# A Strassen-Winograd feed-forward layer on one core: three of the seven first-layer products of the last two groups as two-level units

## The chip, the core and the metric

The kernel runs on one core of a Trainium2 chip. The metric is device time in microseconds (us), from the first to the last instruction of one execution, as the median of several runs. The engines are named as the profile names them: PE (TensorE, with PEld for its weight loads), DVE (VectorE), ACT (ScalarE), POOL (GpSimd) and SP (the queue that issues most DMAs).

## What is computed

Eight images of 576 tokens go through an efficient attention (softmax of q over its features, of k over the tokens), then a Fourier mix, a layer norm and a feed-forward block:

```python
q_s = softmax(q, axis=-1); k_s = softmax(k, axis=2)
x = q_s @ (k_s^T v)                           # heads joined: (8, 576, 512)
u = x + real(fft(fft(x, axis=1), axis=2))
un = (u - mean) / sqrt(var + 1e-06)
out = u + relu(un @ w_ch1) @ w_ch2            # 512 -> 2048 -> 512
```

All arithmetic on the chip is in float32. The change touches only `relu(un @ w_ch1)`, the first layer, and what stands around it.

## The kernel before

**Groups and orders.** The 4608 tokens are cut into nine groups of 512: groups 0 to 7 are 512 tokens of one image each, group 8 has the left-over tokens of all images. They go through the feed-forward block one after the other, in the order 0 to 6, then 8, then 7. The place in that order is called the order: order 0 is computed plainly, orders 1 to 8 by a Strassen-Winograd scheme of seven products instead of eight. The attention and the Fourier mix of the next image run beside the feed-forward block of the present one, so during orders 1 to 6 PE, DVE, ACT and POOL have work of both. During order 7 only the layer norm of the last group is left, and during order 8 nothing.

**First layer (`up`, L1527 on).** The transposed normalized tokens `unT` (512 features by 512 tokens) and the weights are cut into 2 x 2 blocks. `unT` has seven slots: four raw blocks and three sums, made by DVE and POOL (L1396, L1400, L1405). The weights have seven slots per 128 rows, combined once at the start, kept in DRAM as eight tensors `w1s0` to `w1s7`, and loaded anew for each order, 896 KB at a time, into a ring of four places in `big` (`load`, L476). The loop over `j` takes four quarters of the 2048 columns; for each quarter come seven products in the order 1, 6, 5, 7, 2, 4, 3 (`ORDER`), each of four matmuls of 128 x 128 weights and 256 columns (L1544; the trace has two records for each float32 matmul, so a product shows as x8). Products add up in three PSUM banks `ba`, `bb`, `bc`. `strassen` (L1492) takes them out: ACT copies the first (L1515), DVE makes the sums `u2`, `u3` (L1514) and the four results (L1555), ACT applies the ReLU (L1551, L1556). At the end of a quarter `a_side` (L405 to L408) makes the four sums that the second layer needs: on POOL for orders 1 to 6, on DVE for orders 7 and 8. The results stand in `big`, in seven slots per row block; `hpairs` and `hblock` address them.

**Second layer (`deep_down`, L1641 to L1695, for orders 2 to 8).** Its products are two-level: product 1 and, in order 8, products 2 and 4 are single ones of 256 columns (L1641), the others are units of seven products of 128 columns (L1671), with operands made by `a_step` (L1617), sums taken out at L1678, L1685 and L1692, and results added to the output rows by `into` (L1621) and `sums` (L1624). `into` and `sums` run on POOL for orders 2 to 6, on DVE for 7 and 8 (`E`). The five `into` that follow the last unit, (5, 3), reach into the next order's first layer. The weights of the units, `w2d`, come in loads of 1024 KB.

**What sets the order of work.** Each step is a function with a planned time; all are sorted by it, and each engine issues its own instructions in that order. An engine that waits holds up all that stands behind it on that engine. The planned times are no clock: an instruction whose inputs are there starts at once. One planned unit is 0.87 us.

Of the kernel before, what the change touches and what calls it, by code (L numbers as in the profile page):

```python
# [40 lines left out]
F32 = mybir.dt.float32  # L41
# [78 lines left out]
def at(t, script):  # L120
    return [(t + dt, step) for dt, step in script]
# [17 lines left out]
class _Block:  # L139
    def __init__(self, ctx, tc, q, kT, v, w1, w2, ft, cd, out):  # L140
# [43 lines left out]
        d = self.dram  # L184
        self.w1s = [d.tile([P, 7, HD], F32, tag=f"w1s{p}", name=f"w1s{p}", bufs=1) for p in range(NP)]
        self.w2s = d.tile([7, P, NP, HD], F32, tag="w2s", name="w2s", bufs=1)
# [3 lines left out]
        for at in range(1, B + 1):  # L190
            self.base[at] = len(self.plan)
            self.plan += [self.w1s[p][:].rearrange("p a n -> p (a n)") for pair in PAIRS for p in pair]
# [59 lines left out]
    def flat(self):  # L252
        return self.turned().rearrange("p r n -> p (r n)")
# [163 lines left out]
    def combine(self, layer, p):  # L417
# [19 lines left out]
        if layer == 0:  # L437
            ops = ((4, ALU.add, 2, 3), (2, ALU.subtract, 0, 2), (5, ALU.subtract, 4, 0), (6, ALU.subtract, 1, 5))
            engines, times = (nc.vector,) * 4, (0, 0.4, 0.8, 1.2)
            to, first, second = self.w1s[p][:], slice(0, 2), slice(2, 3)  # L440
            one, two = halves(w[:, p, :]), quarter(3).unsqueeze(1)
# [1090 lines left out]
    def up(self, order, g):  # L1532

        nc, V = self.nc, self.nc.vector
        steps = []
        base, e = self.base[order], V if order >= B - 1 else nc.gpsimd
        for j in range(NP // 2):
# [25 lines left out]
            t = 2 * len(ORDER) * j  # L1563
            steps += at(t, job) + [(t + 2 * len(ORDER) - 0.5 + 5 * i * (j < NP // 2 - 1), lambda n=base + 2 * j + i: self.used(n)) for i in range(2)]
        return steps

# [24 lines left out]
    def deep_down(self, g, order):  # L1591
# [26 lines left out]

        def into(u, d, m):
            x = self.xs[g, u][:, :, d * HD:(d + 1) * HD].rearrange("p c (e n) -> p c e n", n=P)  # L1620
            E.tensor_tensor(out=x, in0=x, in1=tile(m), op=ALU.add)  # L1621
# [58 lines left out]
        def ends(unit, n):  # L1680
# [14 lines left out]
            if n == 3:  # L1695
# [3 lines left out]
                 (7, 6): [(1, sums, 6, 1), (3, into, 0, 1, 6), (5, sums, 7, 6), *(((7, into, 1, 0, 7), (9, into, 1, 1, 7)) if last else ())],  # L1699
                 (5, 3): [(0.6, into, 1, 1, 5), (1.2, into, 0, 1, 5), (1.8, into, 0, 1, 3)] if last else  # L1700
                         [(4, into, 1, 0, 7), (5.5, into, 1, 1, 7), (7, into, 1, 1, 5), (8.5, into, 0, 1, 5), (10, into, 0, 1, 3)]}
# [132 lines left out]
def kernel(ctx: ExitStack, tc: tile.TileContext, q, kT, v, w1, w2, ft,  # L1834
                                                           cd, out):
    blk = _Block(ctx, tc, q, kT, v, w1, w2, ft, cd, out)

    def timed(t, order, g):
        b = order + 1
# [92 lines left out]
    for order, g in enumerate(groups[1:], 1):  # L1932
        later += timed(t, order, g)
        t += UP + (TWICE if order > 1 else UP)
    steps += [(before + scale * t, step) for t, step in later]
# [58 lines left out]
```

## Time and profile before

| what | us |
|---|---|
| median of 3 runs (lowest, highest) | 1006.81 (1006.33, 1007.28) |
| the profiled execution, first to last instruction | 1006.6 |
| PE busy in it | 995.6 |
| DVE / ACT / POOL busy in it | 718.6 / 493.2 / 442.9 |
| first layer of order 7, start to start of its second layer | 815.03 to 863.51 |
| first layer of order 8, start to start of its second layer | 908.37 to 956.72 |

The page of the profile shows no other time of the profiled execution than its span. A row of the timeline gives the start, the duration, the engine, the line, the operation with output and input, its shape and count, and, in brackets, how long the engine had been idle and what ended that. Matmuls overlap in their pipeline, so the time that a product costs is read from the distance of two starts, not from its duration.

### The profile page before, as it was taken

Reading aid. Unit: us, or ns where it says so; the run is one execution under the profiler, and the core shown is the slowest. Engines: PE = TensorE matmul, PEld = TensorE weight load, DVE = VectorE, ACT = ScalarE, POOL = GpSimd, SP = SyncE. Lnnn points to the kernel's source line nnn. Section 1 sums busy time; section 2 is a strip of 40 time slices with the busy share of each in tenths; the row PEclk is TensorE's granted clock in tenths of the full one; section 3 lists DMA queues with packets and bytes.
Section 4 is the critical chain, followed back from the end, with each engine's and each line's share of the span. In section 5 each row is a group of like instructions: output and inputs, shape, how many; then the busy total and the mean of one; then the engine's idle time right before and its main releaser. Section 6 shows DMA issues by size and latency. Waiting matters only on the chain.

```text
span 1006.6 us, 19808 instructions
## 1 busy us (share of the span) xinstructions
PE 995.6 (99%) x7562; PEld 855.7 (85%) x7562; DVE 718.6 (71%) x1356; ACT 493.2 (49%) x1277; POOL 442.9 (44%) x445
## 2 busy tenths in 40 slices
PE   8999999999999999999999999999999999999998
PEld 6844464888888899889988998899889998998897
DVE  6898898666765887588756877688667945685563
ACT  4585642872468228832775177625772342151200
POOL 4263420357535637664655465655646450040000
PEclk9999999999999999999999999999999999999999
DMA  9987499687989666975677577847753765674573
GB/s 300 258 281 245 158 240 346 205 243 226 342 283 272 230 230 219 266 237 210 251 220 242 206 269 237 253 174 270 231 204 135 267 213 200 224 265 172 183 256 132
DMA packets 123559, 236.37 MB, mean 235 GB/s; under 512 B 24184, under 2 KB 88440, under 8 KB 112840
## 3 DMA queue, kind: packets, MB, share of 16 engines
q1 hardware_dynamic: 123096, 234.58, 71.0%
q8 instruction: 60, 0.98, 0.4%
q14 instruction: 35, 0.29, 0.1%
q10 hardware_dynamic: 288, 0.26, 0.1%
q0 software_dynamic: 80, 0.26, 0.1%
HBM read 199.94 MB, written 39.06 MB: 237 GB/s over the span
## 4 chain that ended last, share of the span: by engine, by line
PE 87%; DVE 7%; ACT 3%; DMA 1%; issue 1%; SPq 0%; POOL 0%; DVEq 0%; POOLq 0%
PE bb L1544 16%; PE ba L1544 11%; PE bc L1544 11%; PE bb L1671 10%; PE ba L1671 7%; PE bc L1671 7%; PE bb L1641 5%; PE bc L1479 2%; PE bb L1760 2%; PE two L840 2%; PE one L755 2%; PE two L1207 1%; PE two L1264 1%; PE ba L1479 1%; PE bc L1760 1%; PE ba L1760 1%
## 5 line engine op out<-in xcount | busy, mean ns | idle before, releaser
L1544 PE MATMUL bb<-unT,big 128*128 128x256 f32 x768 | 183.3, 380 | 0.0
L1544 PEld LDWEIGHTS bb<-unT,big 128*128 128x128 f32 x768 | 144.8, 190 | 20.7 <-DVE u L1514 0.7
L1556 ACT ACTIVATE big<-big 128x512 f32<-128x512 f32 x96 | 59.8, 629 | 147.6 <-DVE big L1555 141.0
L1544 PE MATMUL ba<-unT,big 128*128 128x256 f32 x512 | 123.9, 382 | 0.0
L1544 PE MATMUL bc<-unT,big 128*128 128x256 f32 x512 | 121.5, 380 | 0.1
L817 ACT ACTIVATE qT<-q 32x128 f32<-32x128 f32 x384 | 117.9, 307 | 5.9 <-DVE q L807 0.8
L1544 PEld LDWEIGHTS bc<-unT,big 128*128 128x128 f32 x512 | 96.9, 190 | 13.7 <-DVE big L1555 0.5
L1544 PEld LDWEIGHTS ba<-unT,big 128*128 128x128 f32 x512 | 95.5, 190 | 13.9 <-issue 0.5
L1514 DVE TENSOR_TENSOR u<-bb,s 128x512 f32<-128x512 f32 x66 | 45.2, 685 | 85.0 <-PE bb L1544 66.5
L1671 PE MATMUL bb<-big 128*128 128x128 f32 x848 | 103.8, 276 | 0.2 <-DVE u L1678 0.2
L1671 PEld LDWEIGHTS bb<-big 128*128 128x128 f32 x848 | 98.9, 192 | 1.0 <-DVE u L1678 1.0
L1390 POOL COPY unT<-unT 32x256 f32<-32x256 f32 x98 | 42.0, 428 | 90.2 <-DVE unT L1382 85.9
L1621 POOL TENSOR_TENSOR x<-x,big 128x512 f32<-128x512 f32 x45 | 60.9, 1368 | 46.0 <-DVE big L1678 19.7
L1617 DVE TENSOR_TENSOR big<-big 128x512 f32<-128x512 f32 x98 | 79.9, 842 | 0.0
L1671 PE MATMUL ba<-big 128*128 128x128 f32 x640 | 79.0, 276 | 0.0
L1671 PEld LDWEIGHTS ba<-big 128*128 128x128 f32 x640 | 75.0, 192 | 0.8
L1390 ACT COPY unT<-unT 32x256 f32<-32x256 f32 x126 | 50.7, 402 | 31.3 <-DVE unT L1382 29.5
L804 POOL TENSOR_TENSOR q<-q,qm 128x512 f32<-128x512 f32 x24 | 25.8, 1073 | 88.2 <-DVE qm L799 53.1
L405 POOL TENSOR_TENSOR big<-big 128x512 f32<-128x512 f32 x24 | 30.4, 1268 | 68.4 <-ACT big L1556 68.4
L1641 PE MATMUL bb<-big 128*128 128x256 f32 x256 | 58.3, 379 | 0.0
L1555 DVE TENSOR_TENSOR big<-bc,u 128x512 f32<-128x512 f32 x64 | 44.0, 688 | 17.3 <-PE bc L1544 16.4
L1641 PEld LDWEIGHTS bb<-big 128*128 128x128 f32 x256 | 48.0, 190 | 6.1
(336 smaller groups left out, 1917.9 us busy)
## 6 DMA issues: line engine op xcount, KB each, us to landing
big<-w2d SPq DMA_DIRECT2D x67, 1024.0 KB, 4.6
big<-w1s SPq DMA_DIRECT2D x64, 896.0 KB, 4.7
big<-w2s SPq DMA_DIRECT2D x16, 1024.0 KB, 4.8
big<-in_w_dram SPq DMA_DIRECT2D x21, 512.0 KB, 6.0
w2d<-big SPq DMA_DIRECT2D x42, 256.0 KB, 6.5
kb<-in_kT_dram SPq DMA_DIRECT2D x28, 320.0 KB, 7.8
q<-in_q_dram SPq DMA_DIRECT2D x28, 256.0 KB, 6.0
vt<-in_v_dram SPq DMA_DIRECT2D x84, 80.0 KB, 2.7
```

Source lines behind the costliest of these rows:

```text
L405: e1.tensor_tensor(out=to(4), in0=at(2), in1=at(3), op=ALU.add)
L817: nc.scalar.activation(to[t, i * Q:i * Q + Q], one, ACT.Exp)
L1390: copy(to, of)
L1514: plus = lambda t: V.tensor_tensor(out=temp(t), in0=box["bb"][:], in1=box["s1"][:], op=ALU.add)
L1544: nc.tensor.matmul(bank()[:, i, :], lhsT=w[:, WA_AT[m], k * P:(k + 1) * P], rhs=self.unT[g][:, B_AT[m], k, :], start=first and i == 0 and ...
L1555: steps = [(0, lambda: V.tensor_tensor(out=hp(i), in0=bank()[:], in1=u()[:], op=ALU.add)), (0.8, lambda: nc.scalar.activation(hp(i), hp(i) ...
L1556: (0.8, lambda: nc.scalar.activation(hp(i), hp(i), ACT.Relu))]
L1617: e.tensor_tensor(out=to(o), in0=to(x), in1=to(y), op=op)
L1621: E.tensor_tensor(out=x, in0=x, in1=tile(m), op=ALU.add)
L1641: nc.tensor.matmul(box[name][:, i, :], lhsT=h[p][:, A_AT[m], i * P:(i + 1) * P], rhs=self.stream[n][:, p, :], start=p == 0 and (m != 1 or ...
L1671: nc.tensor.matmul(box[place[n]][:, i, :], lhsT=own(m)(A_AT[n])[:, f, :], rhs=w[:, r // 2, r % 2 * P:r % 2 * P + P], start=first and f == ...
L1760: nc.tensor.matmul(bank()[:, i, :], lhsT=h[p][:, A_AT[m], i * P:(i + 1) * P], rhs=w[:, p, :], start=first and i == 0 and p == 0, stop=p == ...
```

## The change

In orders 7 and 8 the first layer is written out anew (`wide_up`).

- Products 1, 6, 7, 5 stay as they were, quarter by quarter, in this order and each in a PSUM bank of its own (`ba`, `bb`, `one`, `bc`).
- Products 2, 3 and 4 are computed for all four quarters at once, each as a unit of a second Strassen-Winograd level (`wide_unit`): seven products of four matmuls with 128 columns. The three units stand behind the four products of the first quarter, and the other three quarters follow them.
- The right sides of a unit, blocks of 128 x 128, need four small subtractions on DVE (`minus`), which read and write SBUF alone. Each unit has five additions from PSUM on DVE (`plus`) and two copies on ACT. Its four results go into slots 5, 6 and 4 of the hidden layer and are added later, by POOL (`more`) or DVE.
- The left sides of the units are loaded once, in the second layer of order 6, from DRAM into tiles that the attention no longer needs (`kb`, `q`, `F`, `ft`, `cd`, `ZT`, `vt`, `qT`, `T`): seven DMAs on SP, 3 MB in all. Their four sums for each unit are made once (`wide_sums`): unit 2's on DVE at the end of order 6, those of units 3 and 4 on POOL in the first layer of order 7, eight additions of 128 x 512.
- The side sums for the second layer run half on DVE, half on POOL (the last quarter's on DVE).
- The five `into` behind order 7's last unit go from DVE to POOL.
- The eight tensors `w1s0` to `w1s7` become one DRAM tensor, in which the part of one `p` has a longer stride between partitions.

The core of the diff:

```diff
+SHORT = (1, 6, 7, 5)
+UNIT, WIDE_AT = 7.2, {2: 5, 3: 6, 4: 4}
+WIDE = 3 * UNIT + 2 * len(SHORT) * (NP // 2)
...
+        self.w1c = d.tile([P, NP, 7, HD], F32, tag="w1s", name="w1s", bufs=1)
+        self.w1s = [self.w1c[:, p] for p in range(NP)]
...
-        base, e = self.base[order], V if order >= B - 1 else nc.gpsimd
+        base, e = self.base[order], nc.gpsimd
+        if order >= B - 1:
+            return self.wide_up(order, g)
...
+    def wide_sums(self, m, e, *times):
+        def make(o, x, y, op):
+            w = self.wide[m]
+            e.tensor_tensor(out=w[o], in0=w[x], in1=w[y], op=op)
+        some = (4, 2, 3, ALU.add), (5, 4, 0, ALU.subtract), (2, 0, 2, ALU.subtract), (6, 1, 5, ALU.subtract)
+        return [(t, lambda a=a: make(*a)) for t, a in zip(times, some)]
...
+    def wide_unit(self, g, m, *at_sums):
+        raw = lambda i: self.unT[g][:, B_AT[m], i // 2, i % 2 * P:i % 2 * P + P]
+        b_at = lambda i: raw(i) if i in (0, 2, 3) else some[:, (4, 1, 5, 6).index(i), :]
+        to = lambda i: self.hblock(WIDE_AT[m], i % 2, 1 - i // 2)
+        place = {1: "ba", 2: "ba", 6: "bb", 4: "bb", 5: "bc", 3: "bc", 7: "one"}
+        def minus(o, x, y):
+            V.tensor_tensor(out=b_at(o), in0=raw(x), in1=raw(y) if y < 4 else b_at(y), op=ALU.subtract)
+        def product(n):
+            for j in range(4):
+                nc.tensor.matmul(box[name][:, j, :], lhsT=self.wide[m][A_AT[n]][:, j, :], rhs=b_at(B_AT[n]),
+                                 start=first and j == 0, stop=True, skip_group_check=True)
+        def ends(n):
+            if n == 1:
+                nc.scalar.copy(temp("s1"), box["ba"])
+            if n == 6:
+                plus(temp("u2"), "bb", "s1")
+            if n == 7:
+                plus(temp("u3"), "one", "u2")
+                plus(to(3), "bc", "u3")
+            if n == 2:
+                nc.scalar.copy(to(0), box["ba"])
+            if n == 4:
+                plus(to(2), "bb", "u3")
+            if n == 3:
+                plus(to(1), "bc", "u2")
+        steps = [(t, lambda o=o, x=x, y=y: minus(o, x, y))
+                 for t, (o, x, y) in zip(at_sums, ((4, 1, 0), (5, 3, 4), (1, 3, 1), (6, 2, 5)))]
...
+            if j == 0:
+                put(1.9, lambda: nc.scalar.copy(hp(0), box["ba"]))
+                put(3.9, lambda: plus(temp("u2"), "bb", own(0)))
+                put(5.9, lambda: plus(hp(1), "one", got("u2")))
+                put(7.9, lambda: plus(hp(3), "bc", own(1)))
+                put(8.7, lambda: plus(hp(2), "bc", got("u2")))
...
+                put(12.7, more, G, 0, own(0), 2)
+                put(15.5, more, G, 2, own(2), 3)
+                put(22.6, more, G, 1, own(1), 4)
+                put(25.2, side, V, 4, 2, 3, ALU.add)
+                put(25.3, side, V, 2, 0, 2)
+                put(26, side, G, 5, 4, 0)
+                put(26.1, side, G, 6, 1, 5)
...
+        t = 2 * len(SHORT)
+        steps = part(0, 0) + at(t, self.wide_unit(g, 2, -3.05, -3, -1.3, -1.2))
+        for m in (3, 4):
+            t += UNIT
+            steps += at(t, self.wide_unit(g, m, -5.2, -5.1, -3.1, -3.0))
+        t += UNIT
+        for j in range(1, NP // 2):
+            steps += part(t, j)
+            t += 2 * len(SHORT)
...
-        def into(u, d, m):
+        def into(u, d, m, E=E):
...
+                 (5, 3): [(4, into, 1, 0, 7, G), (5.5, into, 1, 1, 7, G), (7, into, 1, 1, 5, G), (8.5, into, 0, 1, 5, G), (10, into, 0, 1, 3, G)] if E is V and not last else
...
+        if order == B - 2:
+            steps += [(t + UP + dt, lambda m=m: blk.wide_load(m)) for m, dt in ((2, 4), (4, 12), (3, 25))]
+            steps += at(t + UP, blk.wide_sums(2, blk.nc.vector, 40, 41, 44, 45))
+        if order == B - 1:
+            steps += at(t, blk.wide_sums(3, blk.nc.gpsimd, 10.1, 10.2, 10.3, 10.4) + blk.wide_sums(4, blk.nc.gpsimd, 15.1, 15.2, 15.3, 15.4))
```

More of the change, by code (lines that the diff above doesn't have):

```diff
@@ L439, in combine @@
             engines, times = (nc.vector,) * 4, (0, 0.4, 0.8, 1.2)
-            to, first, second = self.w1s[p][:], slice(0, 2), slice(2, 3)
+            to, first, second = self.w1s[p], slice(0, 2), slice(2, 3)
             one, two = halves(w[:, p, :]), quarter(3).unsqueeze(1)
@@ new lines, in wide_unit, with temp, plus @@
+    def wide_unit(self, g, m, *at_sums):
+        nc, V = self.nc, self.nc.vector
+        box, sums = {}, {}
+        some = self.gap(m - 2)
+        raw = lambda i: self.unT[g][:, B_AT[m], i // 2, i % 2 * P:i % 2 * P + P]
[5 more added lines that the diff above has]
+        def product(n):
+            name, first = place[n], n in (1, 6, 5, 7, 4)
+            if n == 7:
+                box[name] = self.acc((P, D)).rearrange("p (j n) -> p j n", n=P)
+            elif first:
+                box[name] = self.ps.tile([P, 4, P], F32, tag=name, name=name)[:]
+            for j in range(4):
+                nc.tensor.matmul(box[name][:, j, :], lhsT=self.wide[m][A_AT[n]][:, j, :], rhs=b_at(B_AT[n]),
+                                 start=first and j == 0, stop=True, skip_group_check=True)
+        def temp(name):
+            t = self.work.tile([P, 2, HD], F32, tag=name, name=name, bufs=1)
+            sums[name] = t[:].rearrange("p a (e n) -> p (a e) n", n=P)
+            return sums[name]
+        def plus(out, name, t):
+            V.tensor_tensor(out=out, in0=box[name], in1=sums[t], op=ALU.add)
+        def ends(n):
[3 more added lines that the diff above has]
+                plus(temp("u2"), "bb", "s1")
+            if n == 7:
+                plus(temp("u3"), "one", "u2")
[8 more added lines that the diff above has]
+                 for t, (o, x, y) in zip(at_sums, ((4, 1, 0), (5, 3, 4), (1, 3, 1), (6, 2, 5)))]
+        for k, n in enumerate(ORDER):
+            steps += [(1.02 * k, lambda n=n: product(n)), (1.02 * k + 0.9, lambda n=n: ends(n))]
+        return steps
```

100 lines of the change are left out of this document (95 added, 5 removed).

## The prediction

> **What bounds the kernel now.** I read the page's shares first, then busy time by stage, then PE's timeline at the edges of the two stages that the change rewrites. Page, engines and granted clock:
>
> ```profile
> span 1006.6 us, 19808 instructions
> ...
> PE     995.6 (99%) x7562; PEld 855.7 (85%) x7562; DVE 718.6 (71%) x1356; ACT 493.2 (49%) x1277; POOL 442.9 (44%) x445
> ...
> PEclk9999999999999999999999999999999999999999
> ```
>
> Busy time in five stretches: order 6's second layer, then first and second layer of orders 7 and 8:
>
> ```profile
> core 0: us, PE busy (x) PEld busy (x) DVE busy (x) ACT busy (x) POOL busy (x), PEclk, DMA share, GB/s
> 769.80:815.00 45.20, 45.16 (x400) 44.01 (x399) 30.98 (x66) 19.54 (x52) 23.55 (x29) 1.00 0.62 221
> 815.00:863.50 48.50, 48.50 (x226) 42.51 (x226) 23.05 (x34) 11.24 (x19) 6.51 (x5) 1.00 0.53 185
> 863.50:908.40 44.90, 44.73 (x370) 43.70 (x369) 36.40 (x68) 16.87 (x35) 10.38 (x16) 1.00 0.75 270
> 908.40:956.70 48.30, 48.30 (x226) 42.52 (x225) 24.51 (x37) 11.21 (x19) 0.00 (x0) 1.00 0.49 174
> ```
>
> PE never stops: 48.50 of 48.50 us and 48.30 of 48.30, at full clock. So the end moves one for one with PE's work and with every wait that PE is given. DVE is half busy in these stages (23.05 and 24.51 us), POOL nearly idle; room for additions there seems ample. The span is 0.2 us under the median of the runs (1006.81); I work against the span and add 0.2.
>
> **What PE saves.** PE's timeline: starts of first-layer products in order 7, of second-layer units (x16 is two products of four matmuls), and both stages' edges in order 8:
>
> ```profile
> 815.03 1.89 PE L1544 MATMUL ba<-unT,big 128*128 128x256 f32 x8
> 816.76 1.89 PE L1544 MATMUL bb<-unT,big 128*128 128x256 f32 x8
> ...
> 863.51 7.07 PE L1641 MATMUL bb<-big 128*128 128x256 f32 x32
> ...
> 903.01 1.95 PE L1671 MATMUL ba<-big 128*128 128x128 f32 x16
> 904.79 1.95 PE L1671 MATMUL bb<-big 128*128 128x128 f32 x16
> ...
> 908.37 1.89 PE L1544 MATMUL ba<-unT,big 128*128 128x256 f32 x8
> ...
> 956.72 7.07 PE L1641 MATMUL bb<-big 128*128 128x256 f32 x32
> ```
>
> A product of four matmuls of 256 columns costs 816.76 - 815.03 = 1.73 us; eight matmuls of 128 columns cost 1.78, so four cost 0.89. Products 2, 3, 4 over four quarters are 12 x 1.727 = 20.7 us per group (48.35 / 28 = 1.727); three units of seven are 21 x 0.893 = 18.75 us. **PE saves 1.97 us per group, 3.9 us in all**: without any wait the span is 1002.7.
>
> The Trainium skill's page "TensorE: Matmul & The Clock Gate", section "Back-to-back issue gap", speaks against this: the spacing is set by weight load and matmul together, about 81 ns at 128 columns and 131 ns at 512. Read on a straight line (my estimate from that page) 256 columns would cost 98 ns, a unit 28 x 81 against 16 x 98 ns, and the change would lose. The rows above disagree for float32: half the columns cost 0.223 against 0.432 us, so the sum goes by them.
>
> **What the additions cost: the port that DVE and POOL share.** A unit adds five DVE additions from PSUM, four small DVE subtractions on SBUF alone, two ACT copies. By the rows below an addition from PSUM takes 0.69 us (0.61 to the next start), a 128-column one in SBUF 0.29: some 4.2 us of DVE in a unit of 6.25. It fits, if nothing delays DVE. DVE and POOL at the end of order 6's first layer:
>
> ```profile
> 754.31 0.69 DVE L1514 TENSOR_TENSOR u<-bb,s 128x512 f32<-128x512 f32 x1 [1.13 <-PE bb L1544]
> ...
> 762.60 0.29 DVE L1130 TENSOR_TENSOR eo<-eo 128x128 f32<-128x128 f32 x1
> ...
> 764.40 1.33 DVE L1130 TENSOR_TENSOR eo<-eo 128x128 f32<-128x128 f32 x1
> 765.65 0.28 DVE L1129 TENSOR_TENSOR eo<-eo 128x128 f32<-128x128 f32 x1
> 765.96 1.25 DVE L1130 TENSOR_TENSOR eo<-eo 128x128 f32<-128x128 f32 x1
> ```
>
> ```profile
> 754.01 1.27 POOL L407 TENSOR_TENSOR big<-big 128x512 f32<-128x512 f32 x1
> ...
> 764.31 1.27 POOL L405 TENSOR_TENSOR big<-big 128x512 f32<-128x512 f32 x1 [3.39 <-ACT big L1556]
> 765.66 1.40 POOL L406 TENSOR_TENSOR big<-big 128x512 f32<-128x512 f32 x1
> ```
>
> The same 128-column addition takes 0.29 us when POOL is idle and 1.33 and 1.25 us when POOL adds: both end just after POOL's addition does. An addition fed from PSUM (754.31) runs its 0.69 us beside POOL's. So a DVE operation with both inputs in SBUF waits out POOL's current addition; then POOL waits and takes the port again. Two short ones that don't depend on each other pass together (764.40 and 765.65 end within 0.2 us); a dependent one waits out a whole further addition (765.96).
>
> Now order 7. The rows of before around its start, DVE then POOL:
>
> ```profile
> 812.48 0.69 DVE L1396 TENSOR_TENSOR unT<-unT 128x512 f32<-128x512 f32 x1 [1.72 <-POOL unT L1390]
> ...
> 818.75 0.69 DVE L1514 TENSOR_TENSOR u<-bb,s 128x512 f32<-128x512 f32 x1 [2.45 <-PE bb L1544]
> 819.36 1.19 DVE L1405 TENSOR_TENSOR unT<-unT 128x512 f32<-128x512 f32 x1
> 822.14 0.69 DVE L1514 TENSOR_TENSOR u<-bb,s 128x512 f32<-128x512 f32 x1 [1.60 <-PE bb L1544]
> ```
>
> ```profile
> 813.25 1.27 POOL L1396 TENSOR_TENSOR unT<-unT 128x512 f32<-128x512 f32 x1 [0.81 <-DVE unT L1396]
> 814.48 7.19 POOL L1621 TENSOR_TENSOR x<-x,big 128x512 f32<-128x512 f32 x5
> 885.15 4.30 POOL L1390 COPY unT<-unT 32x256 f32<-32x256 f32 x7 [63.49 <-DVE unT L1382]
> ```
>
> Before, POOL adds until 821.67 and then rests. After, eight sums for units 3 and 4 stand right behind the five `into`, their loads long landed; nothing holds them back, so POOL adds without a gap for 13 x 1.33 us and DVE's share, until about 835. In that time DVE's queue has eleven operations on SBUF alone (L1405's and ten `minus`).
>
> *Ahead of it.* Unit 2's four sums, 0.60 us each, run on DVE between 807.7 and 813 among POOL's copies and delay L1396 by some 1.5 us, to 814, and POOL's partner to 814.7-816.0. PE needs the latter for product 6 at 816.76: hidden by 0.8 us, up to 1 us lost if not. The `into` then start at 816.3.
>
> *Unit 2.* DVE adds u2 at 818.75. The first `minus` waits for POOL until 820.3, the second, which depends on it, until 821.7. Product 7's addition runs 821.8-822.4, L1405 waits until 823.1 and ends 823.6, the last two `minus` wait until 824.8 and end 825.1. Only behind them stand the two additions that empty bank `bc` of product 5 (finished at 822.2): done at 826.4. PE wants `bc` for the unit's third product at 815.03 + 4 x 1.727 + 2 x 0.893 = 823.7 and gets it at 826.5: **2.8 us of wait**.
>
> *Units 3 and 4.* The next unit's `minus` pair stands ahead of u3, and u3 ahead of the addition that lets PE's seventh product into `bc`: the same reckoning gives 0.45 us in unit 2's end and 0.75 us in unit 3's. Unit 4 is free, since POOL is done.
>
> **Order 7 waits some 4.0 us** and loses what both groups gain. Least: every wait meets POOL's addition near its end, 2.5 us of waits in unit 2 less 0.9 us that DVE has in hand, 1.6 us. Most: the last two `minus` don't pass together and both later places wait out a full addition, 4.1 + 1.2 + 1.2 = 6.5. I take 4.0, the walk with the row's own durations.
>
> *Order 8* has no sums, and its POOL additions end some 2 us in, ahead of the first `minus`: no wait but at `bc`, where DVE finishes at 8.5 us and PE asks at 8.7; I put 0.2. Quarters 2 to 4 use four banks in turn, so a result may be taken 5.2 us late; POOL has four additions of 1.33 in 6.9 us, which holds. The side sums end 1.2 us later than before against 2.5 us or more until the second layer needs them: 0.1.
>
> *Loads.* Seven DMAs of 512 KB or less stand on SP among the unit loads of order 6:
>
> ```profile
> big<-w2d SPq DMA_DIRECT2D x9, 1024.0 KB, 4.6
> ```
>
> Three times 1 MB at up to 4.6 us; a unit load comes 3 x 3.57 us ahead of its use, so 6 us of slack, and the DMA share is 0.62: nothing, at most 3 us if two meet. The five `into` taken from DVE in order 8, the copies on ACT and the changed DRAM stride are off PE's path: nothing.
>
> **Sum**: 1006.6 - 3.9 + 4.0 + 0.2 + 0.1 = 1007.0, with 0.2 to the median **1007.2**.
>
> **Rivals.** A measurement here tells 0.2% (2.0 us) from no change.
>
> 1. *No standstill at the port* (faster): DVE gets through between POOL's additions, or POOL reaches its sums so late that they miss the first units. Then only 0 to 0.5 us of wait is left: 1003.1. It counts as faster below 1.6 us of wait in order 7. For it: DVE is half idle by the stage's busy time. Against: the 1.33 us rows. The Trainium skill's page "SBUF — State Buffer", section "Who interferes with whom", also has the lock, for a DVE instruction with two SBUF inputs; the rows above agree. Chance 0.20.
> 2. *The port costs more* (slower): POOL takes the port between every two DVE operations, the late pair too. Place: DVE's queue between u2 and the emptying of `bc`; price 1.3 us for each further turn; from 5.6 us of wait in order 7 it is slower: 6.5 us gives 1009.7. Chance 0.22.
> 3. *The loads* (slower): order 6's unit loads come late behind the 3 MB, up to 3 us: 1010. Chance 0.05.
> 4. *The units don't save* (slower): the page's groups of weight loads, by columns that follow,
>
> ```profile
> L1544 PEld LDWEIGHTS bb<-unT,big 128*128 128x128 f32 x768 | 144.8, 190 | 20.7 <-DVE u L1514 0.7
> ...
> L1671 PEld LDWEIGHTS bb<-big 128*128 128x128 f32 x848 | 98.9, 192 | 1.0 <-DVE u L1678 1.0
> ```
>
> are the same for both shapes (190 and 192 ns). If they set the spacing, a matmul of 128 columns would cost the 0.432 us of 256, a unit 12.1 in place of 6.9 us: 31 us more, 1038. The 0.223 us rows are of this very shape: chance 0.01. The skill's page on TensorE, above, has the milder form of it.
>
> Forecast, no change that counts: 0.52. Faster 0.20, same 0.52, slower 0.28. Range: from rival 1's side (least wait, 1.6 us: 1004.6; a little beyond it) to the most, 6.5 us, 1009.7: 1004.0 to 1009.8. The forecast's own range is 1005.2 to 1008.8.
>
> **What would show it.** PE's units at 0.89 us apart in order 8 show the saving; order 8's first layer should take 46.4 to 46.7 us, order 7's some 50.4. In order 7 PE should idle before the third product of unit 2, released by DVE's addition into `bc`, and the `minus` rows should show 0.8 to 1.4 us there and 0.3 in order 8. It is wrong if those `minus` are short, if POOL rests between its `into` and its sums, or if PE waits in order 6.

## The result, and the profile after

The changed kernel takes **1016.2 us** (median of 4 runs, 1016.03 to 1017.86) against 1006.84 us of the kernel before beside it (4 runs, 1006.33 to 1007.28): a ratio of 1.0097 with a 95% interval of 1.0082 to 1.0111. It is slower, and 6.4 us beyond the upper end of the forecast's range (1009.8 us). The profiled run has 1016.25 us, and 1014.3 us from the first to the last instruction: the times of this document are some 2 us longer than that span (run e3 comes back to it).

The page of the changed kernel, the lines that the prediction showed of the one before:

```profile
span 1014.3 us, 20255 instructions
...
PE 991.7 (98%) x7706; PEld 856.1 (84%) x7706; DVE 741.8 (73%) x1395; ACT 499.1 (49%) x1289; POOL 501.7 (49%) x488
```

PE works 4 us less (991.7 against 995.6), and the span is longer all the same. Busy time of the changed kernel by stage: order 6's second layer, then first and second layer of order 7 and the first of order 8:

```profile
core 0: us, PE busy (x) PEld busy (x) DVE busy (x) ACT busy (x) POOL busy (x), PEclk, DMA share, GB/s
768.80:813.99 45.19, 45.16 (x400) 44.01 (x399) 34.45 (x70) 19.54 (x52) 23.55 (x28) 1.00 0.80 280
813.99:868.29 54.30, 47.39 (x298) 43.22 (x296) 36.46 (x52) 13.05 (x23) 34.14 (x26) 1.00 0.51 179
868.29:915.61 47.32, 45.32 (x368) 43.92 (x369) 38.08 (x70) 17.93 (x37) 17.33 (x21) 1.00 0.67 241
915.61:964.37 48.76, 46.55 (x299) 42.90 (x297) 28.18 (x50) 13.04 (x23) 19.68 (x15) 1.00 0.50 177
```

Order 6 is untouched (45.16 of 45.19 us busy, in spite of the loads and of unit 2's sums). Order 7's first layer took 48.48 us and takes 54.30, its second layer 44.86 and 47.32, order 8's first layer 48.35 and 48.76. From order 7's start to the end it is 1014.3 - 813.99 = 200.3 us against 1006.6 - 815.03 = 191.6: these stages lose 8.7 us. The medians differ by 9.4. The 0.6 us between is not traced to a stage; it is less than the start of order 7 differs from one profiled execution to another (815.03 us here before, 813.15 in run e3, which does the same work up to there). PE's busy time is below the length of each of these stages. What it waited for, in the changed kernel (in all, times, longest):

```profile
engine line waited for: us in total, times, longest us
PE bb L1834 <- DVE u L1689: 4.4, 2, 2.2
PE bc L1636 <- DVE big L1689: 2.3, 1, 2.3
PE bb L1864 <- DVE u L1871: 1.5, 2, 1.3
PE bc L1636 <- DVE big L1645: 1.2, 1, 1.2
PE bb L1636 <- DVE big L1645: 1.2, 1, 1.2
PE bb L1864 <- ACT big L1841: 0.5, 1, 0.5
```

L1636 are the units' products, L1834 the second layer's single product, L1864 its units. The three L1636 rows are the kind of wait that the prediction foretold, the first two of them at its very places: the third product of unit 2 and the seventh (the end of unit 2). The third stands not at the end of unit 3, where the prediction had it, but ahead of unit 3's second product, which waits for bank `bb`. The row of L1834 is the one it did not have: twice 2.2 us, once in each group, where the second layer begins. PE's timeline at the places (shown are the products that begin after a wait):

```profile
825.16 1.13 PE L1636 MATMUL bc<-big,kb 128*128 128x128 f32 x8 [2.32 <-DVE big L1689]
...
830.20 1.16 PE L1636 MATMUL bc<-unT,q 128*128 128x128 f32 x8 [1.23 <-DVE big L1645]
...
833.41 1.13 PE L1636 MATMUL bb<-big,cd 128*128 128x128 f32 x8 [1.16 <-DVE big L1645]
...
868.29 7.17 PE L1834 MATMUL bb<-big 128*128 128x256 f32 x32 [2.21 <-DVE u L1689]
```

DVE's rows ahead of the third wait: unit 3's later pair of `minus`, 1.32 and 1.35 us in place of 0.28, and behind them the addition that empties `bb`:

```profile
830.07 1.32 DVE L1627 TENSOR_TENSOR big<-unT 128x128 f32<-128x128 f32 x1
831.31 1.35 DVE L1627 TENSOR_TENSOR big<-unT,big 128x128 f32<-128x128 f32 x1
832.59 0.68 DVE L1645 TENSOR_TENSOR big<-bb,u 128x512 f32<-128x512 f32 x1
```

### The profile page after: what moved, and what is told of

Its sections match the earlier page's. It is cut to its first block, busy times and chain, and to the rows that moved or that the text cites. A ratio compares the mean times of both kernels' runs of the same rounds, so it can differ in the third digit from the quotient of the medians.

```text
span 1014.3 us, 20255 instructions
## 1 busy us (share of the span) xinstructions
PE 991.7 (98%) x7706; PEld 856.1 (84%) x7706; DVE 741.8 (73%) x1395; ACT 499.1 (49%) x1289; POOL 501.7 (49%) x488
## 4 chain that ended last, share of the span: by engine, by line
PE 81%; DVE 10%; ACT 3%; POOL 3%; issue 2%; DMA 1%; SPq 0%; DVEq 0%; POOLq 0%; ACTq 0%
PE bb L1551 12%; PE bb L1864 10%; PE ba L1551 8%; PE bc L1551 8%; PE ba L1864 7%; PE bc L1864 7%; PE bb L1834 5%; PE bc L1484 2%; PE bb L1954 2%; PE two L845 2%; PE one L760 2%; PE two L1212 1%; PE two L1269 1%; PE ba L1484 1%; PE bc L1954 1%
## 5 line engine op out<-in xcount | busy, mean ns | idle before, releaser
L1551 PE MATMUL bb<-unT,big 128*128 128x256 f32 x576 | 137.7, 380 | 0.0
L1551 PEld LDWEIGHTS bb<-unT,big 128*128 128x128 f32 x576 | 108.4, 190 | 15.4 <-DVE u L1519 0.4
L1864 PE MATMUL bb<-big 128*128 128x128 f32 x848 | 103.9, 276 | 1.6 <-DVE u L1871 1.5
L1864 PEld LDWEIGHTS bb<-big 128*128 128x128 f32 x848 | 98.9, 192 | 2.5 <-DVE u L1871 2.5
L1551 PE MATMUL ba<-unT,big 128*128 128x256 f32 x384 | 93.7, 383 | 0.0
L1551 PE MATMUL bc<-unT,big 128*128 128x256 f32 x384 | 91.2, 380 | 0.1
L1563 ACT ACTIVATE big<-big 128x512 f32<-128x512 f32 x72 | 44.7, 628 | 77.8 <-DVE big L1562 71.2
L1519 DVE TENSOR_TENSOR u<-bb,s 128x512 f32<-128x512 f32 x50 | 34.2, 684 | 64.5 <-PE bb L1551 46.0
L1551 PEld LDWEIGHTS bc<-unT,big 128*128 128x128 f32 x384 | 72.5, 190 | 10.4 <-DVE big L1562 0.5
L1551 PEld LDWEIGHTS ba<-unT,big 128*128 128x128 f32 x384 | 71.3, 190 | 10.6 <-issue 0.5
L1864 PE MATMUL ba<-big 128*128 128x128 f32 x640 | 79.0, 276 | 0.0
L1864 PEld LDWEIGHTS ba<-big 128*128 128x128 f32 x640 | 75.0, 192 | 0.8
L1834 PE MATMUL bb<-big 128*128 128x256 f32 x256 | 58.6, 380 | 4.4 <-DVE u L1689 4.4
L1834 PEld LDWEIGHTS bb<-big 128*128 128x128 f32 x256 | 47.8, 190 | 11.2 <-DVE u L1689 5.2
L1864 PE MATMUL bc<-big 128*128 128x128 f32 x416 | 50.7, 275 | 0.0
```

Of the source, the lines that this page charges most:

```text
L1519: plus = lambda t: V.tensor_tensor(out=temp(t), in0=box["bb"][:], in1=box["s1"][:], op=ALU.add)
L1551: nc.tensor.matmul(bank()[:, i, :], lhsT=w[:, WA_AT[m], k * P:(k + 1) * P], rhs=self.unT[g][:, B_AT[m], k, :], start=first and i == 0 and ...
L1563: (0.8, lambda: nc.scalar.activation(hp(i), hp(i), ACT.Relu))]
L1834: nc.tensor.matmul(box[name][:, i, :], lhsT=h[p][:, A_AT[m], i * P:(i + 1) * P], rhs=self.stream[n][:, p, :], start=p == 0 and (m != 1 or ...
L1864: nc.tensor.matmul(box[place[n]][:, i, :], lhsT=own(m)(A_AT[n])[:, f, :], rhs=w[:, r // 2, r % 2 * P:r % 2 * P + P], start=first and f == ...
```

## The experiments

Two theories, each with rivals, were to be told apart. **A, a loop in quarters 2 to 4**: each quarter's first step waits, by way of three engines, for the quarter before, and a turn of this loop takes longer than the quarter's products. **B, the port**: the waits in the units come from DVE's `minus` standing behind POOL's additions, as the prediction had it. **Theory D** put a further 1.7 us on the new DRAM tensor, because the span and the time stood 2.0 us apart in the changed kernel and 0.2 us in the page of the one before.

The loop can be read from the changed kernel's timeline. A quarter's first product in bank `ba` is read twice: ACT copies it (L1731), DVE adds it to slot 5 (L1689 `big<-ba,big`). ACT's rows from quarter 2's ReLUs to quarter 4's copy, then DVE's and POOL's between:

```profile
855.65 1.67 ACT L1702 ACTIVATE big<-big 128x512 f32<-128x512 f32 x3 [5.63 <-POOL big L1696]
857.23 0.57 ACT L1731 COPY s<-ba 128x512 f32<-128x512 f32 x1
858.55 0.63 ACT L1702 ACTIVATE big<-big 128x512 f32<-128x512 f32 x1 [0.76 <-DVE big L1689]
863.45 1.67 ACT L1702 ACTIVATE big<-big 128x512 f32<-128x512 f32 x3 [4.27 <-POOL big L1696]
865.03 0.56 ACT L1731 COPY s<-ba 128x512 f32<-128x512 f32 x1
```

```profile
857.83 0.69 DVE L1689 TENSOR_TENSOR big<-ba,big 128x512 f32<-128x512 f32 x1 [2.71 <-ACT s L1731]
858.43 1.41 DVE L1699 TENSOR_TENSOR big<-big 128x512 f32<-128x512 f32 x2
```

```profile
859.26 1.71 POOL L1699 TENSOR_TENSOR big<-big 128x512 f32<-128x512 f32 x1 [3.64 <-ACT big L1702]
860.93 2.49 POOL L1696 TENSOR_TENSOR big<-u,big 128x512 f32<-128x512 f32 x2
```

Copy (857.23) to DVE's slot 0: 0.60 us; to its side sums: 0.60; to POOL's side sum: 0.83; that one 1.67, the two additions behind it in POOL's queue (L1696) 2.52 until ACT's ReLU of slot 1 may start at 863.45; three ReLUs 1.58; then the next copy, 865.03. The turn takes 7.80 us (the one before it 857.23 - 848.07 = 9.16, with two side sums in POOL's queue) where the products of a quarter take 6.91. No engine but PE is full. (POOL's row names ACT's ReLU at 858.55 as what released the side sum; by the code it reads DVE's sum at 858.43, which ended 0.06 us earlier. Both come behind the copy.) One link is not in the code: DVE's slot 0 doesn't read `s`, yet its idle 2.71 us end with ACT's copy into `s`. The two read the same bank. The Trainium skill's page "PSUM — Partial Sum Buffer", section "PSUM bank collisions raise a hardware error", says that the compiler orders any two engines' accesses to the same bank and quarter of the partitions, reads among them; the row agrees.

All stages below are in us, from PE's timeline: first layer of order 7, its second layer, first layer of order 8. Each ratio is to the kernel before, run beside it on the same chip; its median was 1006.84 to 1007.39 us.

| kernel | median | ratio to before (95%) | 7 first | 7 second | 8 first |
|---|---|---|---|---|---|
| before | 1006.84 | | 48.48 | 44.86 | 48.35 |
| after | 1016.2 | 1.0097 (1.0082 to 1.0111) | 54.30 | 47.32 | 48.76 |
| e1 ReLUs behind copy | 1009.73 | 1.003 (1.0019 to 1.0042) | 51.95 | 45.63 | 46.39 |
| e2 no POOL work | 1012.56 | 1.0062 (1.0045 to 1.0079) | 48.76 | 47.34 | 48.78 |
| e3 before, one DRAM tile | 1007.1 | 1.0003 (0.9993 to 1.0013) | 48.48 | 44.87 | 48.35 |
| e4 loop and sums moved | 1008.97 | 1.0021 (1.0011 to 1.0031) | 46.81 | 45.62 | 46.39 |
| e5 ReLUs, last kept | 1009.76 | 1.0019 (1.001 to 1.0029) | 51.99 | 45.70 | 46.39 |
| e6 sums in gaps | 1006.95 | 0.9994 (0.9985 to 1.0003) | 48.33 | 45.69 | 46.45 |
| e7 last group only | 1006.15 | 0.9988 (0.9979 to 0.9997) | 49.65 | 44.83 | 46.39 |
| e8 differences on POOL | 1004.78 | 0.9981 (0.9972 to 0.999) | 46.61 | 45.70 | 46.39 |
| e9 last group, early load | 1005.04 | 0.998 (0.9971 to 0.9989) | 48.47 | 44.87 | 46.38 |
| e10 only ReLU 1 | 1009.89 | 1.0024 (1.0014 to 1.0034) | 51.96 | 45.76 | 46.39 |
| e11 only ReLU 2 | 1013.72 | 1.0072 (1.0054 to 1.009) | 53.36 | 47.30 | 47.75 |

### e1 and e5: the loop taken apart

```diff
-                put(24.2, relu, 1)
+                put(24.4, relu, 1)
...
-            put(9.5, relu, 2)
+            put(9.95, relu, 2)
...
-            put(8.3, relu, 1)
+            put(10.9, relu, 1)
```

> The changed kernel with one difference: in quarters 2 to 4 the ReLUs of slots 1 and 2 are issued behind the next quarter's copy of s1 (and the first quarter's ReLU of slot 1 behind the second quarter's). Nothing is left out. Theory A (a loop through the quarters: copy of s1 behind ReLU 1, ReLU 1 behind POOL's addition, that behind POOL's side sum, that behind DVE's side sum, that behind DVE's slot 0, that behind the copy; 9.2 and 7.8 us a turn where the products take 6.9): the copies come 6.9 us apart, the two idle stretches of 2.2 us ahead of the second layers' single product go, and with them most of the 1.8 us of new waits in the second layer of the seventh group: 1016.2 - 4.4 - 1.8 = 1010.0 us (1009 to 1012). Rival C (the bank is late because DVE or POOL simply has too much work in the quarters, in whatever order): the idle stretches stay at 2 us or more each, 1015 to 1017 us.

Measured: 1009.73 us, both idle stretches of 2.2 us gone, order 8's first layer 46.39, order 7's second layer 45.63. One thing in this form differs from the changed kernel in more than order: in the last quarter the second layer's first sum then stands ahead of the ReLU of slot 1 that it should follow, so it reads that slot without it. Hence the mended form, in which the last quarter keeps the ReLUs where the change put them (8.3 and 9.5):

> As the first run (ReLUs of slots 1 and 2 behind the next quarter's copy), but in the last quarter, behind which no copy follows, both ReLUs stay where the change has them, so that the second layer's first sum reads slot 1 behind its ReLU. Nothing is left out. Theory A: the loop is gone as before, 1009.7 us, or up to 0.5 us more if that last ReLU had been late. If the gain of the first run came only from the sum that did not wait for the ReLU, the time returns to 1014 us or more.

Measured: 1009.76 us. The gain is not that of the sum. ACT's copies in this kernel:

```profile
854.53 0.59 ACT L1731 COPY s<-ba 128x512 f32<-128x512 f32 x1 [0.43 <-PE ba L1685]
...
861.44 0.59 ACT L1731 COPY s<-ba 128x512 f32<-128x512 f32 x1 [0.42 <-PE ba L1685]
```

They are 6.91 us apart, the products' own pace, and released by PE. What PE still waits for in this kernel:

```profile
engine line waited for: us in total, times, longest us
PE bc L1636 <- DVE big L1689: 2.3, 1, 2.3
PE bc L1636 <- DVE big L1645: 1.2, 1, 1.2
PE bb L1636 <- DVE big L1645: 1.2, 1, 1.2
PE bb L1865 <- DVE u L1872: 0.7, 2, 0.6
```

The port's three waits are untouched, the 4.4 us are gone and so is most of the second layer's (L1864 before, L1865 here). Theory A holds: only the order of ACT's queue was changed. Rival C, too much work in the quarters in whatever order, falls, since no work went.

### e10 and e11: which link

The same diff with ReLU 1 alone, and with ReLU 2 alone.

> Which link closes the loop. The changed kernel with the ReLU of slot 1 alone behind the next quarter's copy of s1 (the last quarter's stays); the ReLUs of slots 3 and 2 stay ahead of the copy. If the loop runs through POOL's addition into slot 1 and that ReLU (theory A), the way over ReLU 2 is short enough (copy to POOL's first addition 4.9 us, to ReLU 2's end 6.4 us, under the 6.9 us of a quarter) and the time is that of the mended run, 1009.8 us (1009 to 1011), without the 2.2 us idle stretches. If the loop runs through slot 2's addition and ReLU 2 as well, they stay at 1 us or more each and the time at 1012 to 1016 us.

> The other half: the ReLU of slot 2 alone behind the next quarter's copy, that of slot 1 stays ahead of it. Theory A: the loop is untouched, both idle stretches of 2.2 us and the waits behind the first of them stay, 1016 us (1015 to 1017.5). If any ReLU less in front of the copy helps, 1010 to 1013 us.

Measured: 1009.89 and 1013.72 us. ReLU 1 closes the loop, as expected. The expectation for ReLU 2 missed: the loop stays, but PE's waits shrink in the second kernel from 4.4 us to

```profile
PE bb L1835 <- DVE u L1689: 2.4, 2, 1.2
```

The loop's own sum fits. ReLU 2 is not a link, but it stands in ACT's queue between ReLU 1 and the copy and lengthens each turn by its 0.5 us: the copies are now 856.20 - 847.56 = 8.64 and 863.49 - 856.20 = 7.29 us apart, in place of 9.16 and 7.80. Two turns, 1.0 us: 2.2 becomes 1.2. In both kernels PE's idle time is what the two turns are longer than the products' 6.91 us, less 0.9: 2.25 + 0.89 - 0.9 = 2.2 in the changed one, 1.73 + 0.38 - 0.9 = 1.2 here.

### e2: the port

```diff
-        if order == B - 1:
-            steps += at(t, blk.wide_sums(3, blk.nc.gpsimd, 10.1, ...) + blk.wide_sums(4, ...))
...
-                nc.tensor.matmul(..., lhsT=self.wide[m][A_AT[n]][:, j, :], ...)
+                nc.tensor.matmul(..., lhsT=self.wide[2][A_AT[n]][:, j, :], ...)
...
-                         [(4, into, 1, 0, 7), (5.5, into, 1, 1, 7), ...]
+                         [] if late else [(4, into, 1, 0, 7), (5.5, into, 1, 1, 7), ...]
```

> The changed kernel with POOL's work beside the first units of the seventh group left out: the eight weight sums of units 3 and 4 (both then read the sums of unit 2, which leaves the number of products the same) and the five additions into x at the end of the sixth group. Theory B (DVE's 128x128 differences take 1.0 to 1.35 us instead of 0.28 because POOL works on the same memory at the time, which makes the units late): all differences take 0.28 to 0.3 us, the three waits of 2.32, 1.23 and 1.16 us ahead of units 2 to 4 go, the first layer of the seventh group takes 54.3 - 4.7 = 49.6 us, the kernel 1016.2 - 4.7 = 1011.5 us, or up to 1 us less where DVE then is less late behind it. Rival (DVE has too many operations ahead of the units, however fast they are): the waits stay over 1 us each and the time within 1 us of 1016.

This form leaves out POOL's eight sums for units 3 and 4, which read unit 2's sums in their place, and the five `into` behind order 6; DVE has the same operations in the first layers as in the changed kernel. Measured: the three waits are gone, order 7's first layer takes 48.76 us, the median is 1012.56. The half of the differences that build on an earlier one, both groups together, first in this kernel and then in the changed one (least, median, most in ns):

```profile
L1627 DVE TENSOR_TENSOR big<-unT,big x12: 284/288/292, 818.9 to 928.9; 128x128 f32<-128x128 f32 x12
```

```profile
L1627 DVE TENSOR_TENSOR big<-unT,big x12: 279/292/1353, 819.4 to 934.1; 128x128 f32<-128x128 f32 x12
```

Theory B holds. The port costs more than the idle time that PE shows, 4.7 us: 54.30 - 48.76 = 5.5 us. After a stop the next product begins with no overlap (0.17 us otherwise) and takes 1.13 us or more in place of 1.06. The loop's 2.2 us and the second layer's 47.3 us stay as they were: the two causes are apart.

### e3: the DRAM tensor

The kernel before, with

```diff
-        self.w1s = [d.tile([P, 7, HD], F32, tag=f"w1s{p}", name=f"w1s{p}", bufs=1) for p in range(NP)]
+        self.w1c = d.tile([P, NP, 7, HD], F32, tag="w1s", name="w1s", bufs=1)
+        self.w1s = [self.w1c[:, p] for p in range(NP)]
```

> The kernel before, with the first layer's weights in one DRAM tile instead of eight; nothing else of the change. Theory D (the change's times grew 9.4 us and its span 7.7 us, and its products ran 0.9 us ahead from the first group on, because of where that tile lies): the time outside the span grows from 0.2 to about 1.9 us, the first group's start comes 0.9 us earlier, the time becomes 1006.8 + 1.7 - 0.9 = 1007.6 us. Rival (both come from somewhere else, such as the number of instructions or chance): 1006.8 us within 0.5, no shift.

Measured: 1007.1 us beside 1007.07 of before. Theory D falls. The spans that come with the times show what misled: in the runs of the kernel before, time and span stand some 1.75 us apart as well (1007.55 and 1005.8, for one), so the execution on the page of before, with its 1006.6, was by this distance one of the longer ones, of some 1008.4 us. Over all runs of all kernels the distance lies between 1.7 and 2.2 us. The late start of order 7 on that page (815.03 against 813.99) belongs to that execution too: it is 813.15 here.

### e4 and e6: sums moved into the sixth group

The loop mended (in e4 in e1's form), and the sums of units 2, 3 and 4 made elsewhere:

```diff
-            steps += at(t + UP, blk.wide_sums(2, blk.nc.vector, 40, 41, 44, 45))
+            steps += at(t + UP, blk.wide_sums(2, blk.nc.vector, 8.0, 8.1, 8.2, 8.3) + blk.wide_sums(3, blk.nc.vector, 40, 41, 44, 45))
+            steps += at(t + UP, blk.wide_sums(4, blk.nc.gpsimd, 24, 24.1, 24.2, 24.3))
...
-        steps = part(0, 0) + at(t, self.wide_unit(g, 2, -3.05, -3, -1.3, -1.2))
+        steps = part(0, 0) + at(t, self.wide_unit(g, 2, -6.4, -6.3, -3.0, -2.9))
```

> The ReLUs moved as in the run with the copy ahead of them, and beside it: the weight sums of unit 2 go on DVE 30 us earlier, those of unit 3 on DVE into the places that unit 2's had, those of unit 4 on POOL between two stretches of the sixth group's second layer where it idles 5.6 us, and the first two differences of unit 2 ahead of the first take-out of u2. Nothing is left out. Theories A and B together: the loop's 6.2 us go and of the 4.7 us ahead of the units at least 4 (the additions into x stay beside unit 2's differences): 1016.2 - 6.2 - 4 = 1006.0 us (1004.5 to 1007.5). If DVE or POOL has no room in the sixth group's second layer, that layer grows by up to 2 us.

Measured: 1008.97 us, 3 us more than expected. Both first layers came out (46.81 and 46.39), but order 6's second layer pays, 48.9 us in place of 45.2: the port again, this time with POOL's sums beside DVE's additions for the Fourier mix. POOL, then DVE, in this kernel:

```profile
785.43 1.51 POOL L1611 TENSOR_TENSOR qT<-q,qT 128x512 f32<-128x512 f32 x1 [1.59 <-DMA qT<-w1s]
```

```profile
784.80 0.42 DVE L1300 TENSOR_TENSOR x<-x,eo 128x255 f32<-128x255 f32 x1
785.13 0.69 DVE L1810 TENSOR_TENSOR big<-big 128x512 f32<-128x512 f32 x1
785.73 1.50 DVE L1299 TENSOR_TENSOR x<-x,eo 128x257 f32<-128x257 f32 x1
787.15 1.48 DVE L1300 TENSOR_TENSOR x<-x,eo 128x255 f32<-128x255 f32 x1
```

0.42 us becomes 1.5 beside POOL's sums, and DVE, which has little room there (94% busy from 784 to 794 in the changed kernel), is late for PE at 796.27 by 2.21 us. The next form puts unit 4's sums where DVE transposes, normalises or rests (two on POOL at 31.4, two on DVE at 36):

> The previous run's ReLUs, and the weight sums placed where no two-input operation of the other engine runs beside them: unit 2's on DVE in its 5.6 us of idle time at the start of the sixth group's second layer, unit 3's on DVE where unit 2's had been, two of unit 4's on POOL between its last sum and the first of its copies while DVE reads PSUM and normalises, the other two on DVE in its 1.4 us of idle time ahead of the transposes; unit 2's first two differences ahead of the first take-out. Nothing is left out. Theories A and B together: the sixth group's second layer as in the kernel before, both first layers at 46.5 us instead of 48.4, the seventh group's second layer at 45.4 us: a span 3.4 us under that of before, 1003.7 us (1002.5 to 1005.5). If DVE's 32 more two-input operations cost even without POOL beside them: 1006 us or more.

Measured: 1006.95 us, no difference from before that counts, and 3 us above the expectation. Two gaps were misjudged: PE waits 0.23 and 0.58 us in order 6's second layer, where one of DVE's sums takes 1.69 us beside POOL's and the transposes come later, and 1.52 us at unit 2's third product, since its `minus`, though earlier now, still run beside POOL's five `into`.

### e7 and e9: the last group alone

Order 7's first layer is again as in the kernel before; order 8 keeps the units, with e5's ReLUs; loads and sums of the units move from order 6 into order 7.

```diff
-        base, e = self.base[order], nc.gpsimd
-        if order >= B - 1:
+        base, e = self.base[order], V if order >= B - 1 else nc.gpsimd
+        if order >= B:
...
+        if order == B - 1:
+            steps += [(t + dt, lambda m=m: blk.wide_load(m)) for m, dt in ((2, 2), (4, 14), (3, 28))]
+            for m, dt in ((2, 16), (4, 30), (3, 44)):
+                steps += at(t + dt, blk.wide_sums(m, blk.nc.gpsimd, 0, 2, 4, 6))
```

> The units for the last group alone, with the ReLUs moved as above; the seventh group's first layer as in the kernel before. The twelve weight sums run on POOL during the seventh group's first layer, two apart each, where POOL has nothing else to do; the three loads are issued there too. Nothing is left out. The saving of one first layer: 48.4 - 46.4 = 2.0 us, so 1007.1 - 2.0 = 1005.1 us (1004.5 to 1006). If POOL's sums slow DVE's side sums of that layer until the products wait, 1006 us or more; the prediction's own view of one layer's saving (1.97 us) stands or falls with this run.

Measured: 1006.15 us. Order 8's first layer takes 46.39 us, but order 7's first layer pays 1.2 us for one wait of 1.04: DVE's side sum beside POOL's sums of unit 2, which had begun late, released by their load. POOL's first of them in this kernel, and below it the row of DVE's side sum (0.69 us in the next quarter):

```profile
824.06 1.27 POOL L1611 TENSOR_TENSOR kb<-kb 128x512 f32<-128x512 f32 x1 [3.66 <-DMA kb<-w1s]
```

```profile
828.50 1.64 DVE L411 TENSOR_TENSOR big<-big 128x512 f32<-128x512 f32 x1
```

In e9 unit 2's load is issued in order 6's second layer (at 25), its sums are planned at 10.5 in place of 16 and without gaps, so that POOL is done before DVE's side sums begin:

> The units for the last group alone as before, with unit 2's load issued in the sixth group's second layer, so that POOL makes these sums before DVE's first side sums of the seventh group's first layer instead of beside them. Nothing is left out. The 1.04 us wait in that layer goes: 1006.15 - 1.1 = 1005.0 us (1004.3 to 1005.8). If that wait had another cause than POOL beside DVE, it stays, and the time with it.

Measured: 1005.04 us, the expectation to 0.1, and 1.9 us faster than the kernel before beside it. Order 7 is back at 48.47 and 44.87 us. This is the change's saving for one group without its price: 48.35 - 46.38 = 1.97 us.

### e8: both groups, the differences on POOL

The mended loop (e5), unit 2's and 3's sums on DVE and unit 2's first two differences earlier, both as in e4 and e6, unit 4's sums on POOL at 12.5 in order 7, and in order 7 the differences on the engine that they had to wait for:

```diff
-            V.tensor_tensor(out=b_at(o), in0=raw(x), in1=raw(y) if y < 4 else b_at(y), op=ALU.subtract)
+            e.tensor_tensor(out=b_at(o), in0=raw(x), in1=raw(y) if y < 4 else b_at(y), op=ALU.subtract)
...
+        t, eng = 2 * len(SHORT), V if order == B else G
```

> The loop mended, and in the seventh group the twelve 128x128 differences on POOL, in turn with its additions into x and the sums of unit 4; sums of unit 2 in DVE's early gap and those of unit 3 where unit 2's had been. Nothing is left out. Theory B in another form: operations of one engine can't hold one another's memory, and DVE's take-outs read PSUM and aren't held, so no wait ahead of the units stays above 0.5 us, though the same differences run beside nothing less than before. Both first layers 46.5 us, the second layer of the seventh group 45.4 us: 1007.1 - 2.0 + 0.5 - 2.0 = 1003.6 us (1002.5 to 1005). If the earlier waits came from the count of operations in front of the units and not from the two engines side by side, POOL, slower than DVE, makes unit 2 late by 2 us or more: 1006 us or more.

Measured: 1004.78 us, ratio 0.9981 (0.9972 to 0.999): **faster than both kernels**, by 2.1 us than before (0.19%, and the interval leaves out 1), 1.2 us short of the expectation. From e9, which has the units in one group alone, it can't be told apart (1005.04): these runs show no gain from the second group. All that PE waits for from order 6's second layer to the end:

```profile
PE bb L1865 <- DVE u L1872: 0.8, 2, 0.6
```

The differences on POOL, and an `into` between them:

```profile
815.07 0.45 POOL L1627 TENSOR_TENSOR big<-unT,big 128x128 f32<-128x128 f32 x1
815.48 1.27 POOL L1815 TENSOR_TENSOR x<-x,big 128x512 f32<-128x512 f32 x1
816.71 0.45 POOL L1627 TENSOR_TENSOR big<-unT 128x128 f32<-128x128 f32 x1
```

0.45 us each but the first (0.90): slower than DVE alone (0.28), some three times as fast as DVE behind POOL (mostly 1.24 to 1.35). e6 is the kernel to compare: its sums of units 2 and 3 and its early differences are the same, its differences are on DVE, and its order 7 has the wait of 1.52 us and 48.33 us for the first layer, against no wait and 46.61 here, although POOL has unit 4's sums to make as well. What is left of the change's price in order 7's stages is its second layer, 45.70 us against 44.86, 0.6 of it in these waits.

## Why the prediction was wrong

The step that failed is the third below: the prediction took the quarters behind the units for free as long as each engine has room, but they hold a loop that is longer than PE's work. The account from order 7's start to the end, by the runs: the saving, 2 x 1.96 = 3.9 us (e8, e9); the port, 5.5 us (after against e2); the loop, 2 x 2.4 us at the start of the second layers (order 8's first layer 48.76 against 46.39; the idle time alone is 2.2) and 1.6 us in order 7's second layer (47.32 against e5's 45.70); 0.8 us more in that layer (45.70 against 44.86). -3.9 + 5.5 + 4.7 + 1.6 + 0.8 = 8.7, what the two profiles differ by.

1. **PE's saving**: right: 1.97 us foretold, 1.97 measured in e9. Where nothing waits, a product of a unit costs 0.89 us, as the rows of the second layer had it.
2. **The port in order 7**: right in mechanism, right in place for two waits of three, mis-sized. The waits were foretold as 2.8, 0.45 and 0.75 us and are 2.32, 1.23 and 1.16: 4.7 in place of 4.0. The third is another one than foretold: unit 3's later pair of `minus` did not pass together, as unit 2's did, but took 1.32 and 1.35 us and held up the emptying of `bb`; the wait foretold at unit 3's end did not come. And each stop costs PE some 0.3 us more than its idle time, which the sum did not have: 5.5 us.
3. **"Quarters 2 to 4 use four banks in turn, so a result may be taken 5.2 us late; POOL has four additions of 1.33 in 6.9 us, which holds"**: this is the step that failed. It compared POOL's work with the time, and there is room. It did not ask whether a quarter's first step waits for the last step of the quarter before, and it does, through ACT's queue: a turn of 7.8 to 9.2 us. Lateness that grows by 0.9 us or more a turn uses up any slack. Nor did it count that DVE's slot 0 waits for ACT's copy out of the same bank. For the quarters behind the units the prediction booked 0.1 us, for the side sums; the runs show 4.7 + 1.6 = 6.3 (e1, e5).
4. **The second layer of order 7** was booked at nothing beyond the side sums. 1.6 us came with the loop, 0.8 us remain with the loop mended, 0.6 of it waits for DVE's additions that empty the banks; the rest is not settled.
5. **Order 8 without the port, the loads and unit 2's sums at nothing**: right. Order 8's `minus` take 0.28 to 0.45 us, its units never wait (the 0.2 us put on its bank `bc` did not come), and order 6's second layer is as it was.
6. **The span 0.2 us under the median**: a coincidence of one execution, by e3's runs; time and span stand 1.75 us apart there. It moved nothing in the forecast but the 0.2 us to the median, since that went by differences. In the range, 1004.6 us for the least wait leaves out the 0.2 us of order 8, which the upper end has in; it would be 1004.8.

A chance of 0.28 stood on slower, none of it for this cause. The two rivals nearest in time were the port at its dearest (1009.7) and the loads (1010), both more than 6 us short; the port was dearer than forecast by 1.5 us, the loads cost nothing that shows. There was no rival for the loop.

## What to carry to other kernels

When a scheme in stages is rewritten, walk one result through every queue from one turn to the next, and compare that length, not the busy times, with the time of a turn; an instruction that waits on another engine and stands ahead of the next turn's first step closes such a loop. Putting it behind that step cost nothing here and took 6.3 us off these stages. Two-input operations of DVE and POOL on SBUF should be counted as one resource, in whatever stage they are moved to; short ones may be better off on the slower engine if that one holds the port, as in e8. A saving on the bounding engine is what is left after both: here 2.0 us with one group (e9) and no more that can be told with two (e8).

## What the runs showed of the hardware

A stop of PE may be followed by some 3.4 us at half clock, and not each time. The wait of 2.3 us ahead of unit 2's third product was followed by full clock in the changed kernel and e5, by half in e1, e10 and e11; the 2.2 us ahead of the second layers (twice in the changed kernel, twice in e2) never was. The granted clock is the third number from the end, in the changed kernel and then in e1:

```profile
824.00:826.00 2.00, 0.83 (x7) 0.86 (x8) 1.43 (x3) 1.10 (x2) 2.00 (x2) 1.00 1.05 254
826.00:828.00 2.00, 2.00 (x20) 2.00 (x19) 1.97 (x3) 0.00 (x0) 2.00 (x3) 1.00 0.87 295
```

```profile
824.00:826.00 2.00, 1.11 (x5) 1.14 (x6) 1.43 (x4) 1.10 (x2) 2.00 (x3) 0.73 1.08 294
826.00:828.00 2.00, 2.00 (x12) 2.00 (x11) 1.97 (x3) 0.00 (x0) 2.00 (x2) 0.50 0.88 313
828.00:830.00 2.00, 2.00 (x18) 2.00 (x18) 1.95 (x4) 0.53 (x1) 1.92 (x3) 0.91 0.92 345
```

Taken as half clock, the means 0.73, 0.50 and 0.91 make 1.08 + 2.00 + 0.36 = 3.4 us. The three products that follow the wait start 1.80 and 1.69 us apart in e1, 0.97 and 0.89 us in the changed kernel. In e1 it cost nothing, since DVE caught up meanwhile and the wait of 1.23 us behind it went (51.95 us for the layer in e1, 51.99 in e5). e4 shows the same behind its wait of 2.21 us (one x16 row of 3.18 us in place of 1.95, granted clock 0.74 and 0.50), as a part of the 3.7 us that order 6's second layer loses there. The Trainium skill's page "TensorE: Matmul & The Clock Gate", section "What's actually happening", has a free-running window of about 3.4 us and half clock after an idle one, and its section "Why this matters for your kernels" advises against gaps over about 3 us. A free-running window would fit that the same gap has either end, but no run here shows it; the length doesn't fit: gaps of 2.2 and 2.3 us were enough here, in four cases of ten.
